# Moving the next chunk's gate arithmetic and block transposes inside a fused mLSTM and feed-forward kernel

## The chip, the cores and the metric

The kernel runs on one core of a Trainium2 chip. The metric is the device time of one execution in microseconds (us). The core has five engines with an instruction queue each: TensorE (PE in the profile, with its weight loads as PEld), VectorE (DVE), ScalarE (ACT), GpSimd (POOL) and SyncE (SP), which issues nearly all of this kernel's transfers.

## The reference

Two stages, all in 32-bit floats. The first is an mLSTM cell over 4 batches, 8 heads, 768 time steps and head size 40; the second is a feed-forward block over the 3072 resulting rows of 320 numbers, with 2048 hidden columns and the quick form of gelu.

```python
for t in range(S):
    m_new = np.maximum(f_gate[:, :, t] + m, i_gate[:, :, t])
    f_stab = np.exp(f_gate[:, :, t] + m - m_new)
    i_stab = np.exp(i_gate[:, :, t] - m_new)
    m = m_new
    C = f_stab[:, :, None, None] * C + i_stab[:, :, None, None] * np.einsum('bhd,bhe->bhde', vt, kt)
    n = f_stab[:, :, None] * n + i_stab[:, :, None] * kt
    h_tilde = np.einsum('bhde,bhe->bhd', C, qt)
    denom = np.maximum(np.abs(np.einsum('bhd,bhd->bh', n, qt)[:, :, None]), 1.0)
    y[:, :, t] = h_tilde / denom / (1.0 + np.exp(-o_gate[:, :, t]))
x = y.transpose(0, 2, 1, 3).reshape(B * S, H * D)
h = x @ w_in
out = (h * (1.0 / (1.0 + np.exp(-1.702 * h)))) @ w_out
```

## The kernel before

**Chunks.** The 768 time steps are cut into six chunks of 128 (w = 0 to 5), so a chunk holds 512 rows, 128 for each batch. The attention of a chunk is computed in closed form with matmuls, and the running state is carried to the next. The main loop (lines 929 to 999) walks the chunks: it does the *first product* (x times w_in, with the gelu) and then the *second product* (times w_out) of chunk w, and threads the attention of chunk w + 1 through the blocks of the second product. The instructions of each engine stand in the order in which the Python code emits them.

**The first product of chunks 1 to 5.** A scheme of seven block products in place of eight is used: the x side and the w_in side are combined beforehand (`token_sums` on VectorE, lines 679 to 684), and the products are put together afterwards. `up_fast(w, j)` does pair j of eight; a pair is 256 hidden columns in two 128-row tiles. TensorE computes products 1 to 7 (L722) into four areas of PSUM, which are called p1 (product 1), p56 (products 5 and 6), row0 (products 2 and 3) and row1 (products 4 and 7). For j = 0 and 4 it also runs `row_product` (L701), which adds the last 64 rows of the inner dimension into the row areas of four pairs at once, in the order j, j + 2, j + 3, j + 1. ScalarE copies p1 to SBUF (L761). VectorE adds p56 to it (L762, L763), then row1 (L774, L775), where L775 writes the second half of the hidden tile g. For pairs 0 to 5 ScalarE copies row0 into g (L739) and GpSimd adds the sums to it (L781); for pairs 6 and 7 VectorE does this (L783). The activation of pair j (L690, two instructions) is emitted in pair j + 1, after that pair's L763.

**PSUM.** It has eight banks here. The pool `ps_m` has four buffers of one bank and serves p1, p56 and the row areas of pairs 0, 1, 4 and 5; the pool `ps_a` has two buffers of two banks and serves the row areas of pairs 2, 3, 6 and 7. A new tile takes a buffer of its pool, and its first writer waits for the last user of the tile that was there. Which buffer it gets is decided when the program is built.

**The next chunk's preparations.** They are emitted between the pairs of the first product, for w = 1 to 4:

- `gates(w + 1)`, L288 to L326: 13 VectorE instructions on small tiles (two scans along time and their differences) and five transfers to DRAM, issued on SP (on GpSimd where `gates` is called for chunk 1): m_row (three; L304, L307), st_row (L330) and d_row (L331).
- `load(w + 1, "o")`: the output gates, eo (L122, on SP).
- after pair 2: `load` of v and k (L117), `columns_in` (L350 to L352), which reads st_row and d_row back in another layout as raw, and `spread` (L403), which reads m_row back into wt.
- `block_transposes(w + 1, n)`, n = 0 to 7 (L394): one VectorE transpose each, of a batch's keys (even n, k_sq to kT) or queries (odd n, q_sq to qT). They are shared out over the pairs by a table. k_sq and q_sq were loaded during the second product before.
- after pair 7: `columns_turn` (L356), a transpose of raw.
- `hidden_difference` after pairs 2 to 5 and `hidden_sums` after pairs 6 and 7 work on the hidden tiles on GpSimd; the last two `hidden_sums` (L820, L823) run on VectorE after the activation of pair 7.

**The second product.** `down_fast` makes seven block products for each half of the rows (L844), with VectorE's adds (L847, L849). The second block needs the hidden tiles of pairs 4 to 7 in order, so its last four matmuls need the activation of pair 7. Chunk 0 uses the plain `up` and `down`.

Of the kernel before, what the change touches and what calls it, by code (L numbers as in the profile page):

```python
# [26 lines left out]
def kernel(  # L27
# [205 lines left out]
    def convert(n):  # L233
        convert_begin(n)
        convert_end(n)
# [32 lines left out]
    def split(engine, dst, x, left, part):  # L268

        first, second, third = (dst[j * BH:(j + 1) * BH, :] for j in range(3))  # L270
        engine.tensor_copy(out=first, in_=x)
        engine.tensor_tensor(out=left, in0=x, in1=first, op=OP.subtract)
        engine.tensor_copy(out=part, in_=left)
        A.copy(out=second, in_=part)
        engine.tensor_tensor(out=left, in0=left, in1=part, op=OP.subtract)
        engine.tensor_copy(out=third, in_=left)

    def side_queue(w):

        return G if w == 1 else nc.sync  # L280

    def gates(w):
        m = m_at[w]
        swapped = gate.tile([3 * BH, L], FP, bufs=1, name="f_run")
        f_run = swapped[0:BH, :]
        m_run = gate.tile([BH, L], FP, bufs=1, name="m_run")
        st = stacked[w] = gate.tile([3 * BH, L], FP, bufs=1, name="st")
        V.tensor_tensor_scan(out=f_run, data0=ones, data1=f_sb[w], initial=0.0, op0=OP.mult, op1=OP.add)  # L288
        a = st[0:BH, :]
        V.tensor_tensor(out=a, in0=i_sb[w], in1=f_run, op=OP.subtract)  # L290
        if w == 0:
            room = work.tile([L, H, D1], FP, tag="u", name="room").rearrange("p h d -> p (h d)")
            neg, part = room[0:BH, 0:L], room.bitcast(BF)[0:BH, 2 * L:3 * L]
            V.tensor_tensor(out=neg, in0=f_run, in1=i_sb[w], op=OP.subtract)
            split(G, a3, neg, neg, part)
        V.tensor_tensor_scan(out=m_run, data0=ones, data1=a, initial=m, op0=OP.mult, op1=OP.max)
        if w == 0:

            room = work.tile([L, H, D1], FP, tag="u", name="room").rearrange("p h d -> p (h d)")
            left, part = room[0:BH, 0:L], room.bitcast(BF)[0:BH, 2 * L:3 * L]  # L300
            split(V, m3, m_run, left, part)
        else:
            to = m_row[w] = rows.tile([2, BH, HL], FP, name="m_row")
            side_queue(w).dma_start(out=to[:, 0::2].rearrange("n h t -> h n t"),  # L304
                              in_=m_run[0::2].rearrange("h (n t) -> h n t", t=HL))
            for n in range(2):
                side_queue(w).dma_start(out=to[1 - n, 1::2], in_=m_run[1::2, n * HL:(n + 1) * HL])  # L307
        end = m_run[:, L - 1:L]
        if w + 1 < NW:
            m_at[w + 1] = gate.tile([BH, 1], FP, name="m_end")  # L310
            V.tensor_tensor(out=m_at[w + 1], in0=f_run[:, L - 1:L], in1=end, op=OP.add)

        mid = m_run[:, HL - 1:HL]
        for x, (old, new) in enumerate(((m, mid), (mid, end)) if w else ((m, end),)):
            t = slice(x * HL, x * HL + HL) if w else slice(0, L)
            V.tensor_scalar(out=st[BH:2 * BH, t], in0=m_run[:, t], scalar1=old, scalar2=None, op0=OP.subtract)
            V.tensor_scalar(out=st[2 * BH:3 * BH, t], in0=a[:, t], scalar1=new, scalar2=-1.0, op0=OP.subtract,
                            op1=OP.mult)
        if w:
            for x in range(2):  # L320
                V.tensor_scalar(out=swapped[:, x * HL:(x + 1) * HL], in0=st[:, (1 - x) * HL:(2 - x) * HL], scalar1=odd,
                                scalar2=None, op0=OP.mult)
            V.scalar_tensor_tensor(out=swapped, in0=st, scalar=even, in1=swapped, op0=OP.mult, op1=OP.add)
            both = gate.tile([BH, 2], FP, name="both")
            V.tensor_tensor(out=both[:, 0:1], in0=m, in1=mid, op=OP.subtract)
            V.tensor_tensor(out=both[:, 1:2], in0=mid, in1=end, op=OP.subtract)  # L326
            st_row = rows.tile([L // 32, 3 * BH, 32], FP, name="st_row")
            d_row = rows.tile([BH, 2], FP, name="d_row")
            stacked[w] = st_row, d_row
            side_queue(w).dma_start(out=st_row.rearrange("n k t -> k n t"), in_=swapped.rearrange("k (n t) -> k n t", t=32))  # L330
            side_queue(w).dma_start(out=d_row, in_=both)  # L331
# [250 lines left out]
    def scale(w, c, part=0, parts=1):  # L582
        n = PH // parts
        hs = slice(c * PH + part * n, c * PH + (part + 1) * n)
        if part == 0:
            vw[w, c] = work.tile([L, PH, D1], FP, tag="u", name="vw")
        e = cols[w][:, 2 * BH + hs.start:2 * BH + hs.stop].unsqueeze(2).to_broadcast([L, n, D1])
        G.tensor_tensor(out=vw[w, c][:, part * n:(part + 1) * n], in0=v_st[:, hs, :], in1=e, op=OP.mult)

    def wait_for(x):  # L590

        G.tensor_copy(out=mark, in_=x[:, 0:1])
# [271 lines left out]
    def run(calls):  # L864
        for f, *args in calls:
            f(*args)
# [62 lines left out]
    for w in range(NW):  # L929
        more = w + 1 < NW  # L930
        if w == 0:
            for j in range(NF // 2):
                if j % 2 == 0:
                    ahead, behind = converted[j // 2]
                    run([(convert, p) for p in ahead] + [(fetch, p) for p in fetched.get(j // 2, ())])
                    up(w, j, lambda: run([(columns_turn, 1) if p is None else (convert, p) for p in behind]))
                if j == 6:
                    load(1, "o")
                if j == 1:
                    wait_for(w_in_sb[:, 1, 512:1024])  # L940
                    scale(0, 1)
                    load(1, "v")
                if j < B and j % 2:
                    carry(0, j // 2)
                if j == 3:
                    masks()
                    gates(1)
                    columns_in(1)
                if j == 4:
                    spread(1)  # L950
                    load_squares(1, "q")
                if j >= B:
                    transposes(1, j - B)
        else:
            token_sums(w)
            if more:
                gates(w + 1)
                load(w + 1, "o")
            for j in range(NF // 2):
                up_fast(w, j)  # L960
                if w == 1 and j < 4:
                    weight_sums(j)
                if more and j == 2:
                    load(w + 1, "vk")
                    columns_in(w + 1)
                    spread(w + 1)
                if more and j:
                    for n in ((), (0, 2), (4,), (6, 1), (3,), (5, 7), ())[j - 1]:
                        block_transposes(w + 1, n)
                if more and j == 7:  # L970
                    columns_turn(w + 1)
                if 2 <= j < 6:
                    hidden_difference(w, j - 2)
                if j >= 6:
                    hidden_sums(w, (j - 6,), G)
            gelu_fast(w, NF // 2 - 1)
            hidden_sums(w, (2, 3), V)
        side = attention(w + 1) if more else {}
        if w == 0:

            blocks = [(lambda b=b, n=n: down(w, b, n)) for n0 in (0, 2) for b in range(B) for n in (n0, n0 + 1)]
        else:
            blocks = down_fast(w, 0) + down_fast(w, 1)
        for i, block in enumerate(blocks):
            if w == 0 and i in (0, 4, 5):
                convert((17, 18, 19)[max(i - 3, 0)])
                if i == 0:
                    for n in (1, 3, 5, 7):
                        block_transposes(1, n)
            if w + 2 < NW and i == (6 if w == 0 else 0):  # L990
                load_gates(w + 2)
            if w + 2 < NW and i == 13:
                load_squares(w + 2, "kq" if w else "k")
            if w == 0 and i == 15:
                load_squares(w + 2, "q")
            block()
            run(side.get(i, []))
            if w == 0 and i in (11, 13):
                input_sums(slice(0, 4) if i == 11 else slice(4, 8))
# [30 lines left out]
```

## Time and profile before

| what | value |
|---|---|
| time, median of three runs | 470.21 us (469.51 to 472.56) |
| the profiled execution's own time | 469.33 us |
| span of the profiled execution | 467.6 us |
| busy TensorE, VectorE, ScalarE, GpSimd | 456.5, 343.3, 186.0, 163.2 us |
| matmuls in the trace | 5071 |
| mean granted TensorE clock | 1.0 |

The profile is one execution, seen by the hardware profiler. "Busy" is the time in which an engine worked; its share of the span says how near the engine is to being the bound, averaged over stages that have different limits. The chain of waits is followed backwards from the last instruction, at each step to what released it; an engine other than the busiest in that chain marks a place where the busiest one stood still. A line of a timeline gives the start, the duration up to the last instruction of the group, the engine, the source line, the operation with output and input, the count, and in brackets the idle time before it with its releaser. Ends of matmuls are modelled, so that starts are the better measure.

### The profile page before, as it was taken

What the parts mean: (1) busy time and instruction counts of PE and PEld (TensorE: products, weight loads), DVE (VectorE), ACT (ScalarE), POOL (GpSimd) and SP (SyncE); (2) the same over time, 40 slices, a digit from 0 to 9 for tenths busy, and PEclk for the clock granted to TensorE, in tenths of its full rate; (3) what the DMA queues carried; (4) which work ended last, traced back from release to release, by engine and by line L of the source; (5) the groups of instructions that cost most, each with busy time, mean ns of one, the idle gap of its engine ahead of it and who ended that gap; (6) DMA issues with size and microseconds to landing.
All of it is one profiled execution on the core that took longest, in us unless ns stands there. A gap on an engine that the chain in (4) does not pass through costs nothing.

```text
span 467.6 us, 12393 instructions
## 1 busy us (share of the span) xinstructions
PE 456.5 (98%) x5071; PEld 388.7 (83%) x5071; DVE 343.3 (73%) x738; ACT 186.0 (40%) x433; POOL 163.2 (35%) x153
## 2 busy tenths in 40 slices
PE   8999999999999999999999999999999999999997
PEld 6867877775878998778999778899888899787996
DVE  6788999799679777698875688876777866553712
ACT  5686779000556500545700353900354720064200
POOL 5101508000997500356700256610148620146200
PEclk9999999999999999999999999999999999999999
DMA  8999999049993045995024997114999405100000
GB/s 165 204 300 210 207 252 186 3 106 208 155 125 90 18 105 127 178 145 115 3 66 126 197 132 134 32 44 113 182 133 120 95 17 135 34 1 1 1 28 29
DMA packets 135561, 52.87 MB, mean 113 GB/s; under 512 B 101984, under 2 KB 131632, under 8 KB 135504
## 3 DMA queue, kind: packets, MB, share of 16 engines
q1 hardware_dynamic: 127136, 50.27, 55.8%
q10 hardware_dynamic: 8048, 1.66, 1.8%
q8 instruction: 40, 0.66, 0.6%
q0 software_dynamic: 320, 0.15, 0.2%
q14 instruction: 17, 0.14, 0.1%
HBM read 44.52 MB, written 7.54 MB: 111 GB/s over the span
## 4 chain that ended last, share of the span: by engine, by line
PE 80%; DVE 12%; DMA 2%; ACT 2%; issue 2%; SPq 1%; DVEq 0%
PE p_out L844 30%; PE p_h L722 20%; PE p_h L626 6%; PE p_out L790 6%; PE p_h L701 5%; PE p_c L602 3%; PE p_o L503 2%; PE p_s L459 2%; PE p_i L511 2%; DVE qT L394 2%; PE p_h L635 2%; ACT g L690 2%; DMA k_sq<-in_k_dram 2%; DVE g L775 1%; DVE parts L763 1%
## 5 line engine op out<-in xcount | busy, mean ns | idle before, releaser
L781 POOL TENSOR_TENSOR g<-g,parts 128x512 f32<-128x512 f32 x30 | 38.2, 1273 | 197.3 <-DVE parts L763 98.8
L761 ACT COPY parts<-p_h 128x256 f32<-128x256 f32 x40 | 14.9, 372 | 156.6 <-PE p_h L722 120.6
L844 PE MATMUL p_out<-w_out_sb,g 128*128 128x160 f32 x480 | 70.0, 301 | 4.1 <-ACT g L690 4.1
L844 PEld LDWEIGHTS p_out<-w_out_sb,g 128*128 128x128 f32 x480 | 66.5, 190 | 5.5 <-ACT g L690 5.1
L722 PE MATMUL p_h<-xT,w_in_sb 128*128 128x256 f32 x240 | 65.9, 383 | 0.0
L690 ACT ACTIVATE g<-g 128x512 f32<-128x512 f32 x80 | 47.8, 630 | 33.1 <-DVE g L775 26.8
L722 PEld LDWEIGHTS p_h<-xT,w_in_sb 128*128 128x128 f32 x240 | 44.6, 190 | 11.9 <-ACT g L739 2.3
L849 DVE TENSOR_TENSOR o_sb<-o_sb,p_out 128x160 f32<-128x160 f32 x70 | 21.4, 317 | 40.7 <-PE p_out L844 40.1
L844 PE MATMUL p_out<-t_sb,s 128*128 128x160 f32 x320 | 47.1, 300 | 0.0
L844 PEld LDWEIGHTS p_out<-t_sb,s 128*128 128x128 f32 x320 | 44.4, 190 | 0.2
L762 DVE TENSOR_TENSOR t_x<-p_h,parts 128x256 f32<-128x256 f32 x40 | 16.8, 421 | 37.8 <-PE p_h L722 26.4
L722 PE MATMUL p_h<-t_x,s_in 128*128 128x256 f32 x160 | 41.4, 381 | 1.4 <-DVE g L775 1.4
L435 ACT ACTIVATE wt<-wt,cols 128x64 f32<-128x64 f32 x160 | 38.8, 333 | 0.1
L701 PE MATMUL p_h<-xT,w_in_x 64*128 64x512 f32 (+1 forms) x200 | 37.1, 514 | 0.0
L722 PEld LDWEIGHTS p_h<-t_x,s_in 128*128 128x128 f32 x160 | 30.1, 190 | 6.9 <-PE p_h L722 1.6
L790 PE MATMUL p_out<-w_out_sb,g 128*128 128x320 f32 x128 | 35.7, 436 | 0.0
L739 ACT COPY g<-p_h 128x512 f32<-128x512 f32 x30 | 17.5, 582 | 39.8 <-PE p_h L701 16.7
L790 PEld LDWEIGHTS p_out<-w_out_sb,g 128*128 128x128 f32 x128 | 23.9, 190 | 9.6
L701 PEld LDWEIGHTS p_h<-xT,w_in_x 64*128 64x128 f32 x200 | 18.5, 186 | 14.9 <-issue 14.1
L626 PE MATMUL p_h<-xT,w_in_sb 128*128 128x256 f32 x128 | 29.6, 384 | 0.0
L775 DVE TENSOR_TENSOR g<-p_h,parts 128x512 f32<-128x512 f32 x40 | 27.6, 691 | 1.4
L626 PEld LDWEIGHTS p_h<-xT,w_in_sb 128*128 128x128 f32 x128 | 23.6, 190 | 5.3 <-issue 2.4
(204 smaller groups left out, 847.5 us busy)
## 6 DMA issues: line engine op xcount, KB each, us to landing
q_sq<-in_q_dram SPq DMA_DIRECT2D x20, 320.0 KB, 10.2
wt<-m_row SPq DMA_DIRECT2D x20, 256.0 KB, 6.1
k_sq<-in_k_dram SPq DMA_DIRECT2D x16, 320.0 KB, 6.1
out_dram<-o_sb SPq DMA_DIRECT2D x24, 160.0 KB, 1.9
eo<-in_o_gate_dram SPq DMA_DIRECT2D x5, 640.0 KB, 8.2
bits<-in_moe_w_in_dram SPq DMA_DIRECT2D x6, 512.0 KB, 10.6
q_sq<-x_row SPq DMA_DIRECT2D x10, 256.0 KB, 2.9
v_st<-in_v_dram SPq DMA_DIRECT2D x14, 160.0 KB, 5.2
```

The source lines that it names most:

```text
L435: A.activation(out=x[:, h, :], in_=x[:, h, :], func=AF.Exp, scale=-1.0, bias=cols[w][:, c * PH + h:c * PH + h + 1])
L626: T.matmul(ph[j][i][:, t], w_in_sb[:, c, f * 128:(f + 1) * 128], x[:, c, t], start=(first and c == 0 and n == 0), stop=(not first and c == ...
L690: A.activation(out=gs[w, j][:, i, :], in_=gs[w, j][:, i, :], func=AF.Gelu_apprx_sigmoid)
L701: T.matmul(row[:, t], w_in_x[r, j, :], xT[w][r, 2].rearrange("p b t -> p (b t)")[:, t], start=(start and h == 0), stop=(not start and h == ...
L722: T.matmul(out, a, x[n], start=start, stop=stop)
L739: A.copy(out=g[:, 0, :], in_=row0)
L762: V.tensor_tensor(out=u2, in0=p56[:, right], in1=y[:, left], op=OP.add)
L775: V.tensor_tensor(out=g[:, 1, :], in0=row1, in1=y[:, half_w:3 * half_w], op=OP.add)
L781: G.tensor_tensor(out=g0, in0=g0, in1=u, op=OP.add)
L790: T.matmul(po, gs[w, f // 2][:, f % 2, b * L:(b + 1) * L], w_out_sb[:, f, :], start=(f == 0), stop=(f == NF - 1))
L844: T.matmul(po, a(f), b[:, f, :], start=(f == 0), stop=(f == NH - 1))
L849: V.tensor_tensor(out=dst, in0=x, in1=po, op=OP.add)
```

## The change

The call of `gates(w + 1)` goes from before `load(w + 1, "o")` and pair 0 to after pair 0. In the table of block transposes the pairs move forward: before, two each were emitted after pairs 2, 4 and 6 and one each after pairs 3 and 5; now two are emitted after pairs 1, 2 and 4 and one after pairs 3 and 5, with none after pairs 6 and 7. All instructions stay; their order changes on VectorE and on SP, where eo's transfer now stands ahead of the five of the gates. Only chunks 1 to 4 are touched.

```diff
         else:
             token_sums(w)
             if more:
-                gates(w + 1)
                 load(w + 1, "o")
             for j in range(NF // 2):
                 up_fast(w, j)
+                if more and j == 0:
+                    gates(w + 1)
                 if w == 1 and j < 4:
                     weight_sums(j)
                 if more and j == 2:
@@
                 if more and j:
-                    for n in ((), (0, 2), (4,), (6, 1), (3,), (5, 7), ())[j - 1]:
+                    for n in ((0, 2), (4, 6), (1,), (3, 5), (7,), (), ())[j - 1]:
                         block_transposes(w + 1, n)
                 if more and j == 7:
                     columns_turn(w + 1)
```

## The prediction

> **What bounds the kernel now.** I read the page's busy line first, then the chain of waits, then TensorE's timeline at each place where the chain leaves TensorE, then VectorE's and ScalarE's timelines there.
>
> ```profile
> PE 456.5 (98%) x5071; PEld 388.7 (83%) x5071; DVE 343.3 (73%) x738; ACT 186.0 (40%) x433; POOL 163.2 (35%) x153
> ```
>
> TensorE is busy for 98%, so a change that leaves its instructions alone can win only its gaps. The chain (start, duration) shows two of them in chunk 2:
>
> ```profile
> 185.10 0.42 DVE f_run L288
> ...
> 187.59 0.42 DVE f_run L321 x2
> 188.52 0.40 DVE t_x L762
> 188.94 0.42 DVE parts L763
> 189.73 0.70 DVE g L775
> 190.56 11.94 PE p_h L722 x54
> ...
> 214.41 0.68 DVE g L783
> 215.08 2.00 DVE qT L394 x2
> 217.44 0.42 DVE parts L763
> 218.23 0.70 DVE g L775
> 218.95 1.24 ACT g L690 x2
> 220.23 5.16 PE p_out L844 x36
> ```
>
> The next chunk's gates (L288 to L326) run on VectorE ahead of pair 0's sums, and two transposes (L394) run ahead of pair 7's; both times TensorE waits for what is queued behind. Its timeline in chunk 2 has the size (brackets: idle time and releaser):
>
> ```profile
> 189.41 0.70 PE L722 MATMUL p_h<-xT,w_in_sb 128*128 128x256 f32 x2
> 190.56 1.10 PE L722 MATMUL p_h<-t_x,s_in 128*128 128x256 f32 x4 [0.45 <-DVE g L775]
> ...
> 202.43 3.70 PE L701 MATMUL p_h<-xT,w_in_x 64*128 64x512 f32 x16
> 206.06 0.70 PE L722 MATMUL p_h<-xT,w_in_sb 128*128 128x256 f32 x2
> 206.60 1.03 PE L722 MATMUL p_h<-t_x,s_in 128*128 128x256 f32 x4
> ...
> 215.23 3.97 PE L844 MATMUL p_out<-w_out_sb,g 128*128 128x160 f32 x28
> 220.23 0.81 PE L844 MATMUL p_out<-w_out_sb,g 128*128 128x160 f32 x4 [1.03 <-ACT g L690]
> ```
>
> Product 5 follows product 1 by 0.54 us where nothing waits (206.06 to 206.60) and by 1.15 at 189.41: a stall of 0.61. In chunks 1, 3 and 4 the same pair of starts gives 0.61, 0.49 and 0.31 (116.23 to 117.38, 262.55 to 263.58, 335.60 to 336.45). Sum: 2.0 us. At the tail, 28 matmuls of L844 take 3.81 us at the undisturbed pace (chunk 5: 30.44 us for 224), but the 29th starts 5.00 after the first: 1.19 lost, and the same in chunks 1, 3 and 4. Sum: 4.8 us. Chunk 5, which has neither gates nor transposes in its first product, shows neither stall. All that can be won is 6.8 us.
>
> **What the Trainium skill says.** "PSUM — Partial Sum Buffer", section "Engine vs sequencer instructions": the queues of ScalarE, VectorE and GpSimd are strict FIFO. The trace agrees: pair 0's L762 starts at 188.48, as the last gate instruction ends, though its matmuls were done by 185.0. Same page, section "PSUM bank collisions raise a hardware error": accesses are to be guarded by bank. So a product into a bank waits for the last reader of whatever tile was there; product 5 at 190.56, released by L775 of the pair before, is such a wait. "Perfetto Trace Analysis", section "Optimization Strategy": find the gaps of the engine that should be saturated and the semaphore that ends each. That is the method here.
>
> **Gates behind pair 0.** No instruction is added. The 13 VectorE instructions, 185.10 to 188.48, are 3.4 us. Without them pair 0's L762 starts at 185.1; L774 must wait for row 1 of the row product (about 187.0), and L775 ends at about 188.1. Product 5 of pair 1 could start at 189.41 + 0.54 = 189.95: 1.8 us of margin, so the 2.0 us go. The gates then take 188.1 to 191.5. Pair 1's L762 started at 191.77 before, on its matmul; gates now end just in time.
>
> Its transfers: SP issues eo's first and the gates' five after it. m_row, issued first of these, still lies before the spread at pair 2; L435, the reader of wt, has about 2.3 us of slack, since its product waits on VectorE (L462 at 231.08) longer than on GpSimd (L439, done at 228.77). st_row and d_row slip to about 194 and 196 on SP, but columns_in's loads stood behind v's and k's until 209.2 anyway. In chunk 4, the tightest, they land at about 362 for L356 at 363.5. Cost: nothing, with 1.3 us to go.
>
> **Transposes one pair forward.** A transpose is 1.04 us (two: 2.08 at 215.00). Each pair up to 5 still has at most two ahead of its successor, and pairs 6 and 7 have none. The pair (0,2), new behind pair 1: pair 1's L775 ends at about 193.4, the transposes at 195.5, pair 2's L762 has its matmul at about 195.8. Cover: 0.3 to 0.4 us; k_sq must be there by 193.4 and landed by about 190.6. q_sq, first needed behind pair 3 at about 201, landed by 197.6. At the end pair 7's L762 starts when its matmul allows, about 214.3 instead of 216.91, and the activation of pair 7 ends at about 217.5, against 218.3 when the 29th L844 wants it: margin 0.8 us. So the 4.8 us go.
>
> **What is late next.** The buffers of a PSUM pool are given out by when the program's builder reckons them free, so the move changes who inherits which bank. I built both programs and resolved each matmul's waits. Outside the first products nothing changes. Between pairs 4 and 5 it does: row 1 of pair 5 (the last four matmuls of L701) took the bank that VectorE's L763 of pair 4 releases, and now takes the one that ScalarE's copy L739 of pair 4 releases. In chunk 1 alone, the two banks p1 and p56 of pair 5 also become one, so that product 5 waits for the copy L761 of product 1. ScalarE in chunk 2:
>
> ```profile
> 204.44 0.63 ACT L690 ACTIVATE g<-g 128x512 f32<-128x512 f32 x1 [0.59 <-POOL g L781]
> 204.97 0.57 ACT L739 COPY g<-p_h 128x512 f32<-128x512 f32 x1
> ```
>
> and in chunk 1:
>
> ```profile
> 132.19 0.57 ACT L739 COPY g<-p_h 128x512 f32<-128x512 f32 x1
> 133.63 0.37 ACT L761 COPY parts<-p_h 128x256 f32<-128x256 f32 x1 [0.88 <-PE p_h L722]
> ```
>
> The last four of L701 want the bank 2.68 us after the first (twelve of sixteen in 3.63 us): 205.11. L739 ends at 205.54, and about 0.1 passes to the start of a waiting instruction: a new stall of 0.5. In chunk 1 it is 132.76 + 0.1 against 129.26 + 2.68 = 131.94: 0.9. In chunks 3 and 4 the copies end at 278.58 and 351.44 against 278.14 and 351.03: 0.5 each. L739 is late because the activation ahead of it waits for GpSimd's sum of pair 3, which follows VectorE's two transposes behind pair 2; the change leaves two there. The shared bank in chunk 1: product 1 starts at 132.90, L761 at 133.63, for 0.37, plus 0.1: product 5 at +1.2 instead of +0.54, 0.65. Together 0.9 + 0.65 + 3 x 0.5 = 3.05 us. No trace of before shows these waits: from below they cost nothing (if ScalarE runs half a microsecond ahead of its old place), from above twice the sum, 6.1. I take 3.05, since the pairs ahead of it keep their order and their number of transposes.
>
> **Sum.** Minus 2.0, minus 4.8, plus 3.05: minus 3.75. The profiled execution itself took 469.33 (span 467.6 and 1.7 around it), so 465.6; the median of the three runs is 0.88 above, 466.4 by the same step, 0.8% down. About 1% (4.7 us) is what a measurement of this kernel can tell from no change.
>
> **Rivals.**
> - *The bank waits are covered.* Then the whole 6.8 us are won: 463.4. For it: the release is only half a microsecond late, and TensorE's own earlier stall would have delayed it as much. Against it: ScalarE's chain hangs on VectorE and GpSimd, not on TensorE.
> - *The tail's gain is taken by another wait.* The 29th L844 needs pair 7's activation, with only 0.8 us of margin, and L356's columns in chunk 4 have 1.3 before they hold VectorE's next sums. If one of them is late by 0.6 in each chunk, 2.5 us return: 468.9. For it: the slim margins. Against it: the activation's own chain starts from TensorE's product, which nothing delays.
> - *Slower.* The two transposes behind pair 1 don't fit. If VectorE reaches pair 2's sums 2.1 us late and never catches up until pair 5, the new ScalarE wait grows by that in four chunks: 8.4 more, so plus 4.65: 474.9. It decides when the transposes end more than about 0.4 us past 195.8 and the idle time of VectorE in pairs 2 to 4 doesn't absorb it. For it: VectorE has two transposes behind pair 2 as well, with only 0.1 us between L763 of pair 3 and TensorE (201.3 against 201.43). Against it: k_sq is 2.8 us early and pair 1 needs no more VectorE time than pair 2.
>
> **Numbers.** Forecast 0.50, covered 0.22, tail partly lost 0.18, slower 0.10. The range, 462.9 to 469.9, holds the first three with the ends of the bank cost inside (463.4 to 469.5) and leaves out the last. Faster by over 1% (under 465.5): most of the covered case and a sixth of the first, 0.28. Slower by over 1% (over 474.9): 0.08 of the last. The rest, 0.64, is within.
>
> **What would show it.** Right: no idle time at product 5 of pair 1 nor ahead of the 29th L844; new idle time on TensorE ahead of the last four of L701 between pairs 4 and 5, named ACT L739, of 0.5 to 0.9, and in chunk 1 a second at product 5. Wrong: L690 still the releaser at the 29th L844, idle time in pairs 2 to 4 that VectorE ends, or a transpose that waits for a DMA.

## The result: no measurable change, and the profile after

The changed kernel takes 469.75 us (median of 20 runs, 468.36 to 472.07) against 469.79 us before (20 runs); the ratio is 0.9992, with a 95% interval of 0.9978 to 1.0006. The forecast gain of 0.8% is not there. (469.75 lies just inside the range of 462.9 to 469.9 that the prediction gave, but not for the reasons that it gave.) The profiled execution took 470.63 us, 0.9 above its own median, with a span of 468.9. Two of the runs below had one execution each in a slower state, with a lower granted clock; their medians and all ratios leave it out.

The busy line of its page:

```profile
PE 459.3 (98%) x5071; PEld 390.7 (83%) x5071; DVE 352.9 (75%) x738; ACT 185.8 (40%) x433; POOL 164.1 (35%) x153
```

TensorE is as full as before. VectorE has the same 738 instructions, and yet 9.6 us more busy time. That is the first trace of something that the prediction did not have. The second is in TensorE's waits (engine and line, what it waited for: us in total, times, longest):

```profile
PE p_h L722 <- DVE parts L763: 2.2, 2, 1.1
PE p_i L511 <- DVE wt L462: 1.4, 3, 0.7
...
PE p_h L722 <- ACT parts L761: 0.5, 1, 0.5
```

Of before's two entries, the activation L690 (4.1 us) and L775 (1.4 us), neither is left. TensorE's timeline at the places shown for before:

```profile
192.00 0.70 PE L722 MATMUL p_h<-xT,w_in_sb 128*128 128x256 f32 x2
192.53 1.03 PE L722 MATMUL p_h<-t_x,s_in 128*128 128x256 f32 x4
...
204.51 4.27 PE L701 MATMUL p_h<-xT,w_in_x 64*128 64x512 f32 x16
...
217.89 4.51 PE L844 MATMUL p_out<-w_out_sb,g 128*128 128x160 f32 x32
```

Product 5 follows product 1 by 0.53 us where it was 1.15, and the 32 matmuls of L844 run as one piece where the last four had stood apart. In their place L701 of pair 4 has grown from 3.70 to 4.27 us. So both stalls went and others came.

From the starts of the first L722 and the first L844 of each chunk one gets the length of each stage in us (a first product with no stall is chunk 5's 31.83):

| chunk | first product before | after | second product before | after |
|---|---|---|---|---|
| 1 | 32.74 | 36.38 | 40.56 | 39.42 |
| 2 | 32.60 | 32.64 | 40.56 | 39.71 |
| 3 | 32.48 | 32.67 | 40.56 | 40.34 |
| 4 | 32.32 | 32.50 | 40.54 | 39.87 |

The second products win 2.9 us; the first products lose 4.05, of which 3.64 in chunk 1. (Before, the four first products were 2.8 us above chunk 5's length in all. The prediction counted start stalls of 2.0; the rest are shorter waits that it left out of what can be won.) The chain of waits runs through VectorE in chunk 1:

```profile
116.44 5.39 PE p_h L722 x24
121.83 0.14 DVE both L325
121.97 0.07 DVE both L326
122.04 0.34 DVE t_x L762
122.41 0.44 DVE parts L763
122.89 1.15 PE p_h L722 x4
124.04 0.69 PE p_h L722 x2
124.77 1.13 DVE kT L394
...
130.11 0.43 DVE parts L763
130.59 1.13 PE p_h L722 x4
131.72 4.28 PE p_h L701 x16
```

L325 and L326 are the last two instructions of the gates. They end at 122.04, seven microseconds after the gates began. VectorE's timeline shows which of them are long (the first two lines are those of before), and GpSimd's shows what ran beside them in the changed kernel:

```profile
111.97 0.41 DVE L288 TENSOR_TENSOR_SCAN f_run<-one,fi 32x128 f32<-32x128 f32 x1
112.41 0.28 DVE L290 TENSOR_TENSOR st<-fi,f_run 32x128 f32<-32x128 f32 x1
```

```profile
115.00 1.51 DVE L288 TENSOR_TENSOR_SCAN f_run<-one,fi 32x128 f32<-32x128 f32 x1
116.55 2.81 DVE L290 TENSOR_TENSOR st<-fi,f_run 32x128 f32<-32x128 f32 x1
119.39 0.47 DVE L296 TENSOR_TENSOR_SCAN m_run<-one,m_end,st 32x128 f32<-32x128 f32 x1
```

```profile
114.98 1.26 POOL L781 TENSOR_TENSOR g<-g,parts 128x512 f32<-128x512 f32 x1 [34.28 <-ACT g L739]
116.21 3.01 POOL L803 TENSOR_TENSOR t_sb<-w_out_sb 128x1280 f32<-128x1280 f32 x1
```

Before, GpSimd had nothing to do beside L288 and L290 (its first L781 of chunk 1 started at 116.71). Each of the two now ends 0.1 to 0.3 us after a GpSimd instruction ends.

The third change is on SP, here in chunk 2, before and after:

```profile
190.46 0.60 SPq L304 DMA_DIRECT2D m_row<-m_run  x1
```

```profile
193.16 0.41 SPq L122 DMA_DIRECT2D eo<-in_o_gate_dram  x1
193.66 8.62 SPq L304 DMA_DIRECT2D m_row<-m_run  x1
```

The issue of m_row behind eo takes 8.6 us (0.6 before). ScalarE's L435 reads wt, which is made from m_row; before it did not wait, and now it does:

```profile
222.19 7.75 ACT L435 ACTIVATE wt<-wt,cols 128x64 f32<-128x64 f32 x32
```

```profile
225.35 7.75 ACT L435 ACTIVATE wt<-wt,cols 128x64 f32<-128x64 f32 x32 [1.83 <-DMA wt<-m_row]
```

From this comes the theory that the experiments test. Three costs eat the gain: VectorE's gates stand still beside GpSimd; the banks of pair 5 wait for ScalarE, as forecast; and eo ahead of m_row makes wt late.

### The profile page after: what moved, and what is told of

Same layout as the page of the kernel before. It is cut to its first block, busy times and chain, and to the rows that moved or that the text cites. A ratio compares the mean times of both kernels' runs of the same rounds, so it can differ in the third digit from the quotient of the medians.

```text
span 468.9 us, 12393 instructions
## 1 busy us (share of the span) xinstructions
PE 459.3 (98%) x5071; PEld 390.7 (83%) x5071; DVE 352.9 (75%) x738; ACT 185.8 (40%) x433; POOL 164.1 (35%) x153
## 4 chain that ended last, share of the span: by engine, by line
PE 78%; ACT 6%; POOL 5%; DMA 4%; DVE 3%; SPq 3%; issue 1%; POOLq 0%; DVEq 0%; ACTq 0%
PE p_out L844 25%; PE p_h L722 21%; PE p_h L701 8%; PE p_out L790 8%; PE p_h L626 6%; ACT wt L435 5%; DMA wt<-m_row 3%; PE p_i L511 2%; PE p_h L635 2%; PE p_o L503 2%; POOL wt L439 1%; PE p_c L602 1%; POOL s L823 1%; DMA s_in<-in_moe_w_in_dram 1%; POOL s L820 1%
## 5 line engine op out<-in xcount | busy, mean ns | idle before, releaser
L781 POOL TENSOR_TENSOR g<-g,parts 128x512 f32<-128x512 f32 x30 | 38.2, 1272 | 197.2 <-ACT g L739 184.7
L761 ACT COPY parts<-p_h 128x256 f32<-128x256 f32 x40 | 14.9, 372 | 156.0 <-PE p_h L722 150.8
L844 PE MATMUL p_out<-w_out_sb,g 128*128 128x160 f32 x480 | 68.9, 300 | 0.0
L844 PEld LDWEIGHTS p_out<-w_out_sb,g 128*128 128x128 f32 x480 | 66.4, 190 | 0.5
L722 PE MATMUL p_h<-xT,w_in_sb 128*128 128x256 f32 x240 | 66.0, 384 | 0.0
L690 ACT ACTIVATE g<-g 128x512 f32<-128x512 f32 x80 | 47.7, 629 | 27.2 <-DVE g L775 22.6
L722 PEld LDWEIGHTS p_h<-xT,w_in_sb 128*128 128x128 f32 x240 | 44.5, 190 | 12.2 <-issue 6.3
L844 PE MATMUL p_out<-t_sb,s 128*128 128x160 f32 x320 | 47.1, 300 | 0.0
L844 PEld LDWEIGHTS p_out<-t_sb,s 128*128 128x128 f32 x320 | 44.4, 190 | 0.2
L722 PE MATMUL p_h<-t_x,s_in 128*128 128x256 f32 x160 | 41.3, 380 | 1.5 <-DVE parts L763 1.1
L435 ACT ACTIVATE wt<-wt,cols 128x64 f32<-128x64 f32 x160 | 38.8, 333 | 6.2 <-DMA wt<-m_row 6.2
L701 PE MATMUL p_h<-xT,w_in_x 64*128 64x512 f32 (+1 forms) x200 | 39.4, 517 | 0.0
L722 PEld LDWEIGHTS p_h<-t_x,s_in 128*128 128x128 f32 x160 | 30.2, 190 | 6.4 <-DVE parts L763 1.5
L762 DVE TENSOR_TENSOR t_x<-p_h,parts 128x256 f32<-128x256 f32 x40 | 17.0, 426 | 24.2 <-ACT g L690 12.7
L701 PEld LDWEIGHTS p_h<-xT,w_in_x 64*128 64x128 f32 x200 | 19.6, 186 | 16.1 <-issue 14.2
L739 ACT COPY g<-p_h 128x512 f32<-128x512 f32 x30 | 17.4, 580 | 38.7 <-PE p_h L701 16.8
L775 DVE TENSOR_TENSOR g<-p_h,parts 128x512 f32<-128x512 f32 x40 | 27.7, 692 | 1.4
L439 POOL TENSOR_SCALAR_AFFINE_SELECT wt<-wt 64x1024 f32<-64x1024 f32 x20 | 23.6, 1178 | 13.2 <-ACT wt L435 12.5
```

What stands on the lines that cost most here:

```text
L435: A.activation(out=x[:, h, :], in_=x[:, h, :], func=AF.Exp, scale=-1.0, bias=cols[w][:, c * PH + h:c * PH + h + 1])
L439: G.affine_select(out=r, in_=r, compare_op=OP.is_ge, fill=0.0, base=0, pattern=[[0, PH], [1, HL]], channel_multiplier=-1)
L690: A.activation(out=gs[w, j][:, i, :], in_=gs[w, j][:, i, :], func=AF.Gelu_apprx_sigmoid)
L701: T.matmul(row[:, t], w_in_x[r, j, :], xT[w][r, 2].rearrange("p b t -> p (b t)")[:, t], start=(start and h == 0), stop=(not start and h == ...
L722: T.matmul(out, a, x[n], start=start, stop=stop)
L739: A.copy(out=g[:, 0, :], in_=row0)
```

## The experiments

Ratios are against the kernel before, measured on the same chip, with 95% intervals. "Stage" lengths are read from starts as above.

**The two parts alone.** First the gates behind pair 0 (and eo ahead of them), with the old table of transposes:

```diff
-                    for n in ((0, 2), (4, 6), (1,), (3, 5), (7,), (), ())[j - 1]:
+                    for n in ((), (0, 2), (4,), (6, 1), (3,), (5, 7), ())[j - 1]:
```

> Gates behind pair 0, transposes where they were before. Theory (three costs: GpSimd holds up the gates' VectorE instructions in chunk 1; a ScalarE copy releases a PSUM bank late between pairs 4 and 5; eo ahead of m_row on SP makes wt late): the start stalls of 2.0 us go, the tail stalls of 4.8 stay, no bank is swapped between pairs 4 and 5 since that comes from the transposes alone, the lateness of wt is hidden behind the tail stall, and chunk 1 loses about 1.1 us because L288 takes about 1.5 us and L290 about 2.8: net -0.9, ratio 0.998, L701 of pair 4 at 3.70 us everywhere. Rival 1 (the gates' move is clean, only the transposes cost): -2.0, ratio 0.9957, L290 at 0.28 us. Rival 2 (the bank waits come with the gates): L701 of pair 4 at 4.3 us here.

It gave 471.47 us, ratio 1.0038 (1.0017 to 1.0058): slower, by 2.6 us more than the theory had it. Either the gates in chunk 1 cost more than 1.1 us, or the tail stall hides less of eo's effect than I took it to. The same kernel with eo behind the gates tells these apart:

```diff
-            if more:
-                load(w + 1, "o")
...
                 if more and j == 0:
                     gates(w + 1)
+                    load(w + 1, "o")
```

> Gates behind pair 0 with the transposes where they were before, and eo behind the gates: the kernel with only the gates moved came out 1.7 us slower than before, where 0.9 faster was expected. Theory (of those, about 1.1 to 1.5 were the late wt behind eo, which the tail stall did not hide, and chunk 1's held-up gates cost 1.9 in place of 1.1): the second products return to 40.56 us, chunk 1's first product stays at 34.6 against 32.7, chunks 2 to 4 win 1.7: about +0.2 on before, ratio 1.000. Rival (eo's place matters only where the tail stall is gone): ratio stays at 1.004.

It gave 469.64 us, ratio 1.0003 (0.9995 to 1.0012), as expected. So about 1.7 us were eo's (the difference of the two ratios, since the runs were on different chips). First products of 31.88, 31.88 and 31.91 us in chunks 2 to 4 show that the start stalls went and that no bank wait came with the gates. The second products are 40.56 us long, and chunk 1's first product is 34.62, 1.9 above before: what the gates win in three chunks they lose in one. TensorE's two waits there:

```profile
122.64 1.13 PE L722 MATMUL p_h<-t_x,s_in 128*128 128x256 f32 x4 [1.09 <-DVE parts L763]
...
134.63 0.70 PE L722 MATMUL p_h<-xT,w_in_sb 128*128 128x256 f32 x2 [0.93 <-ACT g L739]
```

The second is one that I had not counted: ScalarE's copy of pair 4 is late, because GpSimd's queue is, after it had to wait for VectorE's sums of pair 1.

Then the new table alone, in the kernel before:

```diff
-                    for n in ((), (0, 2), (4,), (6, 1), (3,), (5, 7), ())[j - 1]:
+                    for n in ((0, 2), (4, 6), (1,), (3, 5), (7,), (), ())[j - 1]:
```

> Transposes forward, gates and eo where they were before. Theory: the tail stalls of 4.8 us go, the bank waits between pairs 4 and 5 appear (0.57 in each of chunks 2 to 4, and 0.65 + 0.46 in chunk 1: 2.8 together), the start stalls stay, wt is as early as before so no wait of L511, and L290 is 0.28 us: net -2.0, ratio 0.9957. Rival (the transposes behind pair 1 crowd VectorE and are the main loss): chunk 1 loses over 2 us by itself, also without the gates behind pair 0, ratio 1.000 or above.

It gave 468.62 us, ratio 0.9965 (0.9945 to 0.9985), within 0.1% of the expectation. TensorE's timeline in chunks 1 and 2:

```profile
129.51 4.72 PE L701 MATMUL p_h<-xT,w_in_x 64*128 64x512 f32 x16
...
135.32 1.13 PE L722 MATMUL p_h<-t_x,s_in 128*128 128x256 f32 x4 [0.46 <-ACT parts L761]
...
203.25 4.27 PE L701 MATMUL p_h<-xT,w_in_x 64*128 64x512 f32 x16
```

and ScalarE's copy of pair 4 in chunk 2:

```profile
205.78 0.57 ACT L739 COPY g<-p_h 128x512 f32<-128x512 f32 x1
```

The bank waits are those of the prediction, and they come from the table and not from the gates: L701 loses 1.02 in chunk 1 and 0.57, 0.58, 0.57 in chunks 2 to 4, and product 5 of chunk 1 loses 0.62 by its start (134.16 to 135.32, less 0.54). Together 3.4 us, for 3.05 forecast. That the bank makes the wait, and not a later copy, is seen in chunk 2: the copy L739 of pair 4 ends 3.11 us after the first L701 in the kernel before (205.54 less 202.43) and 3.10 here (206.35 less 203.25), and only here do the last matmuls of L701 wait. The rival is out: with the gates in front, the transposes behind pair 1 cost TensorE nothing.

**eo behind the gates**, all else as in the changed kernel:

```diff
-            if more:
-                load(w + 1, "o")
...
                 if more and j == 0:
                     gates(w + 1)
+                    load(w + 1, "o")
```

> The changed kernel with the load of eo behind the gates. Theory: m_row is issued in under 1 us instead of 8.6, wt is not late, the waits of L511 on L462 (0.24, 0.71 and 0.42 us) go; all else stays: about 1.4 us under the changed kernel, ratio 0.996. Rival (wt is late because of all the loads ahead of it on SP, not because of eo): L304 stays at several us or wt lands as late, the waits stay, ratio 0.999.

It gave 468.87 us, ratio 0.9971 (0.9959 to 0.9983), 0.9 under the changed kernel. The expected 1.4 was the idle time in the profiled execution of the changed kernel, which was a long one: its second products of chunks 2 to 4 are 2.0 us longer in all than those of this run. SP's lines in chunk 2:

```profile
193.12 0.61 SPq L304 DMA_DIRECT2D m_row<-m_run  x1
...
199.27 0.40 SPq L122 DMA_DIRECT2D eo<-in_o_gate_dram  x1
```

m_row is issued in 0.6 us, L511 waits no more, and the second products of chunks 2 to 4 are 39.41, 39.26 and 39.24 us long. The runs also lie closer: 468.3 to 469.5, where the changed kernel had 468.4 to 472.1.

One more run exchanges only the two calls in the kernel before:

```diff
-                gates(w + 1)
                 load(w + 1, "o")
+                gates(w + 1)
```

> The kernel before with eo's load issued ahead of the gates' transfers, nothing else. Theory (the transfer behind eo is held on SP for 5 to 9 us, whichever it is): L304 at 5 us or more in place of 0.6, m_row and all behind it later by as much, wt later by some 3 us at L435; the tail stall hides 1.2 us of it, so about 1 us slower, ratio 1.002, and the runs spread wider. Rival (m_row's long issue comes from the gates' later place): L304 at 0.6 us, ratio 1.000.

It gave 469.87 us, ratio 1.0004 (0.9997 to 1.0012). The long issue is there with the gates in their old place too, as the theory had it, but here it costs nothing that can be measured, which the theory had not:

```profile
191.17 0.39 SPq L122 DMA_DIRECT2D eo<-in_o_gate_dram  x1
191.65 8.99 SPq L304 DMA_DIRECT2D m_row<-m_run  x1
```

In chunk 2 L435 starts 8.15 us after the second product does, instead of 6.96 in the kernel before, and the second products are as long as before (40.56 to 40.57). My reading is that SP's stream keeps its own pace, so that this slack shrinks when the first product gets shorter (gates behind pair 0) or the tail stall goes (the new table). It fits the runs, but was not tried by itself.

**GpSimd beside the gates.** The weight sums of chunk 1 (L803) one pair later, in the changed kernel:

```diff
-                if w == 1 and j < 4:
-                    weight_sums(j)
+                if w == 1 and 0 < j < 5:
+                    weight_sums(j - 1)
```

> The changed kernel with GpSimd's four weight sums of chunk 1 each one pair later, so that none runs beside the gates; GpSimd's L781 of pair 0 still does. Theory (VectorE's instructions on two SBUF operands can't go on while GpSimd works on SBUF): L290 in chunk 1 falls from 2.8 to 0.28 us, L288 stays between 1.2 and 1.5 because of L781, the waits of TensorE on L763 in chunk 1 (2.2 us) go: about 2.2 us under the changed kernel, ratio 0.9945. Rival (L290 is long for a reason of its own, a wait on data or a cold start): it stays at 2.8 us and the ratio at 0.999.

The mechanism came out as expected; VectorE's timeline in chunk 1:

```profile
115.28 1.51 DVE L288 TENSOR_TENSOR_SCAN f_run<-one,fi 32x128 f32<-32x128 f32 x1
116.82 0.28 DVE L290 TENSOR_TENSOR st<-fi,f_run 32x128 f32<-32x128 f32 x1
...
146.16 3.31 DVE L820 TENSOR_TENSOR s<-g 128x512 f32<-128x512 f32 x2
149.40 3.46 DVE L823 TENSOR_TENSOR s<-s,g 128x512 f32<-128x512 f32 x2
```

L290 is short again, and the waits on L763 fall from 2.2 to 0.2 us. The time did not follow: 470.34 us, ratio 0.9996 (0.9972 to 1.0021), an inconclusive one. In its profiled execution (468.51 us, a short one: the others go up to 472.1) the first product of chunk 1 won 2.4 us, but its second product lost 0.9. There VectorE's last sums, L820 and L823, take 3.3 and 3.5 us for two each in place of 1.35 and 1.28 before. They start 2.4 us sooner after the start of the chunk than in the changed kernel, while GpSimd's own sums come no sooner, so that GpSimd works beside them. A part of the cost had moved. Why the median won nothing of the 1.5 us that are left is not shown; eo still stands ahead of m_row here.

L288 stayed long, since GpSimd's L781 of pair 0 runs beside it. In one more run that sum is on VectorE:

```diff
-            G.tensor_tensor(out=g0, in0=g0, in1=u, op=OP.add)
+            (G if j else V).tensor_tensor(out=g0, in0=g0, in1=u, op=OP.add)
```

> The changed kernel with the sum L781 of pair 0 on VectorE in place of GpSimd, so that GpSimd does nothing beside the gates in chunks 2 to 4. One look at durations. Theory (VectorE's gates stand still while GpSimd works on SBUF): L288 in chunks 2 to 4 falls from 1.21 us to 0.40, as in the kernel before. Rival (L288 is long behind pair 0 for another reason, such as following instructions that read PSUM): it stays at 1.21.

```profile
189.29 0.41 DVE L288 TENSOR_TENSOR_SCAN f_run<-one,fi 32x128 f32<-32x128 f32 x1
189.74 0.28 DVE L290 TENSOR_TENSOR st<-fi,f_run 32x128 f32<-32x128 f32 x1
```

That is chunk 2. Both are back to their old durations, behind the same pair; the rival is out. In chunk 1, too, where GpSimd now starts only at 121.18, L290 takes 0.28 us, and the gates take 3.3 (116.25 to 119.58), as the prediction had it. (One execution of 466.17 us; only its durations are used.)

**The gates ahead of pair 0 in chunk 1 alone**, with eo behind them everywhere:

```diff
-            if more:
-                load(w + 1, "o")
+            if w == 1:
+                gates(2)
+                load(2, "o")
...
-                if more and j == 0:
+                if more and w > 1 and j == 0:
                     gates(w + 1)
+                    load(w + 1, "o")
```

> The changed kernel with eo behind the gates, and in chunk 1 alone the gates ahead of pair 0 as before, so that nothing of GpSimd's runs beside them. Theory: chunk 1 loses the two waits on L763 (2.2 us), has the start stall of 0.6 again, and the bank wait of L701 at its full 1.0 in place of 0.65: 1.2 us under 468.9, 467.7, ratio 0.9955; chunk 1's first product 34.5 us in place of 36.4. Rival (the waits on L763 come from the two transposes behind pair 1 and not from the gates): they stay, and the start stall is added: 469.5, ratio 0.999.

It gave 466.96 us, ratio 0.9927 (0.9901 to 0.9954): 1.9 us under the kernel that only has eo behind the gates, where 1.2 was expected. Chunk 1's first product is 34.44 us long, as expected. I had counted the waits by their idle times (2.2), which leave out the ends of pipelined matmuls; by the starts of TensorE they were 2.8. The two transposes behind pair 1 stayed, and no wait on L763 is left, so the rival is out.

**The bank waits.** Two ways to take them away, both with eo behind the gates. The first leaves the banks as they are and brings ScalarE's copy of pair 4 forward:

```diff
+        early = apart and k == 0 and j > 0
+        if early:
+            copy_row()
         if j:
             gelu_fast(w, j - 1)
...
-            if k != 2:
+            if k != 2 and not early:
                 copy_row()
```

> The changed kernel with eo behind the gates, and in pair 4 ScalarE's copy L739 ahead of the activation of pair 3 in place of behind it; the banks are given out as in the changed kernel. Theory (the bank wait of pair 5 is L739's lateness, which comes from the activation ahead of it): L701 of pair 4 falls from 4.3 to 3.70 us in every chunk, 0.57 x 3 + 0.65, and the shared bank of chunk 1 still costs 0.5 at product 5: 2.4 us under the kernel that only has eo behind the gates (468.9), 466.5, ratio 0.993. Rival (something else holds up L701, or TensorE meets the next wait at once): L701 stays at 4.3 us, or the time stays within 0.5 us of 468.9.

It gave 467.01 us, ratio 0.9935 (0.9915 to 0.9955), 0.5 above the expectation, though the four first products are 2.3 us shorter in all, as expected. L739 of pair 4 now starts at 205.97, ahead of the activation, in chunk 2, and L701 has its old length in all chunks, while chunk 1's wait on L761 stays:

```profile
132.53 3.70 PE L701 MATMUL p_h<-xT,w_in_x 64*128 64x512 f32 x16
137.33 1.13 PE L722 MATMUL p_h<-t_x,s_in 128*128 128x256 f32 x4 [0.46 <-ACT parts L761]
...
204.81 3.70 PE L701 MATMUL p_h<-xT,w_in_x 64*128 64x512 f32 x16
```

The second leaves the copy and shares the transposes out in another way, for which the builder gives pair 5 the banks that it had before:

```diff
-                    for n in ((0, 2), (4, 6), (1,), (3, 5), (7,), (), ())[j - 1]:
+                    for n in ((0, 2), (4,), (6,), (1, 3), (5, 7), (), ())[j - 1]:
```

> The changed kernel with eo behind the gates, and the transposes shared out as (0,2), (4), (6), (1,3), (5,7) behind pairs 1 to 5: as many ahead of pair 6 as before, but another number behind pairs 2 to 4, with which the builder gives pair 5 the same banks as in the kernel before. Theory (the bank waits are an accident of which bank is given, not of VectorE's load): the waits on L739 and L761 at pair 5 go in all four chunks (0.57 x 3 + 0.65 + 0.6), the waits on L763 in chunk 1 stay: 3.0 us under 468.9, 465.9, ratio 0.9915. Rival (VectorE is too full in pairs 1 to 5 for eight transposes): new waits on VectorE's sums there, ratio over 0.996.

It gave 465.94 us, ratio 0.9915 (0.9894 to 0.9935), the expected figure. With eight transposes still ahead of pair 6, the bank waits are gone. Chunk 1 shows that another bank is given:

```profile
130.79 3.70 PE L701 MATMUL p_h<-xT,w_in_x 64*128 64x512 f32 x16
```

```profile
134.30 0.57 ACT L739 COPY g<-p_h 128x512 f32<-128x512 f32 x1
```

The last four of L701 want their bank at 130.79 + 2.68 = 133.47 and get it, though the copy of pair 4 ends only at 134.87. In chunks 2 to 4 the other table changes the time of the copy as well: one transpose stands behind pair 2 in place of two, and the copy ends 0.3 us before it would be needed (205.69 against 206.00 in chunk 2). There this run alone does not tell the bank from the time of the copy; the comparison of the new table with the kernel before does.

**All together**: eo behind the gates, the other table, and in chunk 1 the gates ahead of pair 0.

```diff
-                    for n in ((0, 2), (4, 6), (1,), (3, 5), (7,), (), ())[j - 1]:
+                    for n in ((0, 2), (4,), (6,), (1, 3), (5, 7), (), ())[j - 1]:
...
-            if more:
-                load(w + 1, "o")
+            if w == 1:
+                gates(2)
+                load(2, "o")
...
-                if more and j == 0:
+                if more and w > 1 and j == 0:
                     gates(w + 1)
+                    load(w + 1, "o")
```

> All three: eo behind the gates, the other table, and in chunk 1 the gates ahead of pair 0. Theory: nothing is left of the three costs; of the 6.8 us of stalls before only chunk 1's start stall of 0.6 stays: 463.7, ratio 0.987. Rival (some of the gain is taken by a wait not yet seen): ratio over 0.990.

It gave 464.00 us, ratio 0.9866 (0.9839 to 0.9892), the expected figure, and faster than the kernel before and the changed kernel. The busy line and two of TensorE's waits:

```profile
PE 455.5 (99%) x5071; PEld 390.2 (84%) x5071; DVE 348.7 (75%) x738; ACT 185.5 (40%) x433; POOL 163.9 (35%) x153
```

```profile
PE p_s L459 <- DVE state L611: 0.7, 1, 0.7
...
PE p_h L722 <- DVE g L775: 0.4, 1, 0.4
```

The first products of chunks 2 to 4 are 31.84, 31.84 and 31.88 us long, those without a stall. What is left in the first products is chunk 1's start stall (L775). The first of the two waits is new, and it is the rival of this run on a small scale: chunk 1's second product takes 40.20 us, where it took 39.41 with the changed kernel's table. VectorE's last sums meet GpSimd there:

```profile
145.03 2.33 DVE L820 TENSOR_TENSOR s<-g 128x512 f32<-128x512 f32 x2
147.29 3.47 DVE L823 TENSOR_TENSOR s<-s,g 128x512 f32<-128x512 f32 x2
```

```profile
147.23 2.98 POOL L588 TENSOR_TENSOR vw<-v_st,cols 128x656 f32<-128x656 f32 x2 [0.42 <-ACT cols L367]
```

With the gates in front in chunk 1 and the changed kernel's table they take 1.35 and 1.28 us. L611, for which L459 waits, stands behind them on VectorE. By this reading the first cost is not gone from this kernel: 0.8 us of it have come back in another place. No run tested that by itself.

A last run had the gates behind pair 0 in chunk 1 too, with the weight sums a pair later in place of the exception (the other table, which it also has, is left out here):

```diff
-            if more:
-                load(w + 1, "o")
...
                 if more and j == 0:
                     gates(w + 1)
+                    load(w + 1, "o")
-                if w == 1 and j < 4:
-                    weight_sums(j)
+                if w == 1 and 0 < j < 5:
+                    weight_sums(j - 1)
```

> Eo behind the gates, the other table, the gates behind pair 0 in chunk 1 too, and there GpSimd's weight sums each one pair later in place of moving the gates back. Theory: L290 is at 0.28 us and the start stall of chunk 1 (0.6) goes as well, but the weight sums end 3 us later on GpSimd, which cost the second product of chunk 1 about 0.9 us in the run that had them later: 464.3 against 464.0 for the kernel with the gates first in chunk 1, ratio 0.987. Rival (those 0.9 us came from the late wt, which is gone): 463.4, ratio 0.9855.

It gave 464.53 us, ratio 0.9887 (0.9870 to 0.9903), near the expectation and no better. Chunk 1's first product fell to 32.15 us (32.68 in the kernel with all together), and its second rose to 41.67, with GpSimd beside L820 and L823 as above.

## Why the prediction was wrong, point by point

- **Both stalls go: right.** Product 5 of pair 1 and the 29th L844 wait no more, in all four chunks. With the three costs away, the kernel is 1.3% faster, as the sum of 6.8 us had it, less chunk 1's 0.6. That this fits so well is partly luck: by stages, the first products win 1.9 us where 1.4 were forecast without chunk 1, and the second products 4.2 where 4.8 were, since chunk 1's gives 0.8 back.
- **The bank waits: right, in place and size.** 3.05 us were forecast, and 3.4 found with the transposes alone. The other table makes 3.0 of difference (466.96 to 464.00), but that is a mixed number: by the traces the first products win 4.0 us with it and chunk 1's second product loses 0.8.
- **"The 13 VectorE instructions, 185.10 to 188.48, are 3.4 us": the step that failed.** The gates' duration was taken along to their new place, and it had been read where GpSimd stood idle. Behind pair 0, GpSimd's L781 runs beside L288 in every chunk, and in chunk 1 L803 runs beside L290 as well. The gates took 4.1 us in chunk 2 (190.63 to 194.76, the start of pair 1's L762), which the margin took in, and 7.0 in chunk 1 (115.00 to 121.97), which it didn't. There VectorE stays behind: with 2.1 us of transposes behind both pair 1 and pair 2 it catches up only in pair 4. Chunk 1's first product is 1.9 us longer for it than with the gates in front (36.38 against 34.44), where 0.6 was to be won: the term is off by 2.5. The trace of before already had a warning: L829, which also reads two operands from SBUF, took 2.24 us for two at 150.33 beside GpSimd's L588 and L579, and 0.75 for two at 156.52.
- **"Cost: nothing, with 1.3 us to go": the second that failed.** I followed the order on SP, and took the duration of each issue with it from where it stood before. The transfer behind eo is held for 4.3 to 9.1 us in chunks 1 to 4 of all traces. Before, that was a load of v (4.68 us in chunk 2), needed late; with eo ahead it is m_row (8.6), behind which the rest of the stream stands. It cost 0.9 us, and about 1.7 in the kernel with the gates alone.
- **The sum.** Minus 6.8, plus 3.05 for the banks, plus 2.5 and 0.9 for the two that were missed: minus 0.35, against a measured ratio of 0.9992, which is minus 0.4 us, with an interval of minus 1.0 to plus 0.3. The terms come from different runs, so that the agreement to a tenth means nothing; that they add up to about nothing does.
- **The rivals.** That the tail's gain is taken by another wait came true in part, but by the wait for wt in the second products and not by either of the two waits that it named. The rival on the slower side named the place where part of it happened, VectorE too late for the sums of pairs 2 to 4, but with the transposes as the cause; with the gates in front these cost TensorE no more at those pairs than before.

What stays open is why a transfer behind eo is held on SP. The traces of all runs show it, and no run changed eo itself.

## What to carry to other kernels

Before moving an instruction, look at what the other engines do at its new place, and not only at what is queued there: a duration read beside an idle GpSimd need not hold beside a busy one, and the time saved at one place can bring the same two engines together at another. The issue of a transfer took 0.6 us or 8.6 here, by what stood ahead of it on its queue; where a chain of work hangs on a transfer, look at what its issue will stand behind. And where a builder gives out buffers, a change of order alone can hand the next tile a buffer whose last user is late: compare who releases each wait in both programs, then size it from the trace.

## What the runs showed of the hardware that I had not expected

VectorE instructions with two operands in SBUF took longer, up to the end of the GpSimd instruction beside them: L290 took 2.81 us beside L803 and 0.28 without it, L288 1.21 to 1.51 beside L781 and 0.41 without, and L820 and L823 took 2.3 to 3.5 us for two each beside GpSimd's sums and L588, and 1.35 and 1.28 without. The Trainium skill, "SBUF — State Buffer", section "SBUF: two separate sides", states this: the port pair that the two engines share is an exclusive lock, held for a whole instruction, which a VectorE operation with two SBUF inputs needs against a GpSimd operation that reads SBUF, so that the later one blocks. The traces agree: L288 starts 0.02 us after L781 and ends 0.27 after it, and L290 ends 0.14 after L803. An operation with one SBUF operand was untouched: a pair of transposes took 2.04 to 2.14 us in every place looked at, beside L803 too (2.10 at 127.65 in the changed kernel).
